# Attention scores through two double-bank buffers in three parts, one maximum a pair, a third score buffer in SBUF

## The chip, the cores and the metric

The kernel runs on one core of a Trainium2 chip. The metric is the device time of one execution in microseconds (us), lower is better. The engines are named as in the profile: PE (matmul) with its weight loads PEld, DVE (vector), ACT (scalar), POOL (GpSimd) and SP, which here only issues DMAs. Each has a queue of its own that runs in order.

## What is computed

A banded attention (8 heads, 4 batches, sequence 768, head size 64) feeds a soft mixture of experts (8 experts with 4 slots each). All in float32, cut to what matters:

```python
def _attn_ref(q, k, v, n_global, n_local):
    scores = scale * np.matmul(q, k.transpose(0, 1, 3, 2))
    rel = pos[:, None] - pos[None, :]
    is_global = pos[None, :] < int(n_global)                 # n_global = 8
    is_local = (rel >= 0) & (rel < int(n_local))             # n_local = 96
    dist = np.where(is_global & ~is_local, float(n_local), np.abs(rel).astype(np.float32))
    scores = np.where(is_global | is_local, scores - slopes[:, None, None] * dist, -1000000000.0)
    a = np.exp(scores - np.max(scores, axis=-1, keepdims=True))
    a = a / (np.sum(a, axis=-1, keepdims=True) + 1e-09)
    return np.matmul(a, v).astype(np.float32)

def _moe_ref(x, phi, w1, w2):
    logits = x @ phi
    d = softmax(logits, over tokens); slot_input = d.T @ x
    slot_out[e] = np.maximum(slot_input[e] @ w1[e], 0.0) @ w2[e]   # 8 experts, 512 -> 1024 -> 512
    return softmax(logits, over slots) @ slot_out
```

(The two softmaxes of the second function are written out in the original.)

## The kernel before

**Work items.** The attention goes over 16 pairs of heads (`units`, numbered u, four pairs a batch; i is the head in the pair). Keys stand on the 128 partitions in seven blocks j of 8 global and 120 local keys. The columns of a block are the queries that can see it, 216 of them (168 and 48 in the last two), so a head's scores are 1296 columns in float32.

**Steps of a pair.** `load_qk` and `load_v` bring q, k and v (two buffers for q and k, one for v). `v_hi` (POOL) and `v_lo` (DVE) split v into two float16 halves. `scores` (line 518) runs 28 PE instructions, both heads side by side, into two PSUM tiles `sc` of three banks each, one a head. `biased` (line 525, DVE) reads a head's 1296 scores, adds the table of distances, writes a float32 buffer (`tp`, four of them, so two pairs) and keeps each partition's maximum. `max_t` (line 533, PE) transposes the maxima into unused columns of a score bank, `max_r` (lines 537 and 538, DVE) reduces and scales them, `max_b` (line 541, PE) spreads the result over the partitions into the same bank and `max_c` (line 545, ACT) copies it out. `exponential` (line 548, ACT) works in place. `w_hi` (line 551, ACT) casts to float16 and `w_lo` (line 555, POOL, in three thirds) writes the rest, also float16, with one buffer of each kind a head. `values` (line 575, PE) multiplies both halves with both halves of v, 39 matmuls a head, into a single bank `x`. `ev_sum`, `ev_rec`, `ev_mul` (lines 580 to 590, DVE) divide by the sum and write `xn`. `tr` (line 603, PE) transposes into a single bank `m` and `tr_copy` (line 608, ACT) takes it out; `logits` (line 633, PE) multiplies with phi through the same bank.

**Once a batch** (u = 3, 7, 11, 15) the strip steps turn the logits into running softmax weights over the tokens and dispatch the batch's tokens to the slots. **After the last pair** come the end of that softmax, the experts' hidden layer (line 106), the projection (line 136), and the combination with the output DMAs.

**Order.** All engines' order comes from one list `ORDER` of steps, written out by hand: each step issues its instructions at its place, and every engine takes its own in that order. `piece` and `free` in that list load the experts' weights: twelve whole pieces of 1 MB into places of their own, the rest into buffers as the attention frees them.

**PSUM before** has eight banks: six for the two score tiles, one for `x`, one for `m`. The lines that keep the maxima in the score banks are

```python
nc.tensor.matmul(out=sc[1][0:2, 1 + z, BW:BW + 64], lhsT=mx, rhs=ident[:, 64 * z:64 * z + 64], start=True, stop=True)
...
nc.vector.tensor_reduce(out=mr, in_=sc[1][0:2, 1:3, BW:BW + 64], axis=AX.XY, op=ALU.max)
```

Of the kernel before, what the change touches and what calls it, by code (L numbers as in the profile page):

```python
# [35 lines left out]
TW = 3 * BW  # L36
PB = KB + P
# [28 lines left out]

# [140 lines left out]
class BiasTable:  # L207
# [66 lines left out]


@with_exitstack
def tile_attention_moe(ctx: ExitStack, tc: tile.TileContext, qk, v, phi, w1, w2, nn, out):
    nc = tc.nc
    const = ctx.enter_context(tc.tile_pool(name="const", bufs=1))
    fast = ExitStack()  # L280
    keep = fast.enter_context(tc.tile_pool(name="keep", bufs=1))
    wk = fast.enter_context(tc.tile_pool(name="wk", bufs=2))
    att = ExitStack()
    ap = att.enter_context(tc.tile_pool(name="ap", bufs=1))
    banks = ExitStack()
# [35 lines left out]
    by_head = "p (j i d) -> p j i d"
    vraw = vt[:, 0:VC].rearrange(by_head, j=NJ, i=2)
    VV = VH + VC // 2
    vhi = [v16[:, VV * i:VV * i + VH].bitcast(F16).rearrange(by_head, j=NJ, i=2) for i in range(2)]
    vlo = [v16[:, VV * i + VH:VV * i + VV].bitcast(F16).rearrange(by_head, j=NJ, i=2) for i in range(2)]
    tabs = [t[:, a:a + TABW].bitcast(BF16).rearrange("p (i c) -> p i c", i=2) for t, a in ((tt, 0), (tt, TABW), (xtt, S), (vt, VC))]
    tbuf = [t[:, 0:TW] for t in tps]
    phi_ = [t[:, TW:].bitcast(F16) for t in tps[0:2]]
    plo_ = [t[:, TW:].bitcast(F16) for t in tps[2:4]]
    xnb = [a[0:KB].rearrange("p (t f) -> p t f", t=NJ) for a in (xn01[:, 0:XH], xn01[:, XH:], xn2[:, 0:XH])]  # L330
    xtb = [xta[:, 0:S], xta[:, S:2 * S], xtt[:, 0:S]]

# [12 lines left out]
    npl = len(places)
    extras = []
    for k, n in enumerate(held):
        at = 0
        for c0, c1 in sorted(c for h, *cs in spaces for c in cs if h == n) + [(WP, WP)]:
            if at < c0:  # L350
                extras.append((NW + k, at, c0))
            at = c1
# [23 lines left out]
    def free(i):  # L376
        n, *cs = spaces[i]
        for c0, c1 in cs:
            load_w([NW + held.index(n)], c0, c1)

# [33 lines left out]
    def blocks(w):  # L414
        return w[:, 0:6 * PB].rearrange("p (s c) -> p s c", c=PB)


    wp = psm.tile([P, 512], F32, name="wp", tag="m")
    busy_in = nc.const_aps.tensor(1.0, [P, 512], BF16)
    for _ in range(WARM):  # L420
        nc.tensor.matmul(out=wp[0:1], lhsT=busy_in[:, 0:1], rhs=busy_in, start=True, stop=True)
# [7 lines left out]
    for i in range(2):  # L429
        nc.gpsimd.memset(vhi[i][:, :, :, D:D + 1], V_SC)  # L430
        for w in (phi_[i], plo_[i]):
            nc.gpsimd.memset(blocks(w)[:, :, QW:], 0.0)
            nc.gpsimd.memset(w[:, 6 * PB:], 0.0)
# [7 lines left out]

    bsel = keep.tile([P, P], F32, name="bsel")
    mms = [keep.tile([P, 2], F32, name=f"mm{i}") for i in range(2)]
    nc.gpsimd.memset(bsel, 0.0)
    nc.gpsimd.memset(bsel[0:3], P_EXP * float(np.log(2.0)))
# [661 lines left out]
```

## Time and profile before

| | |
|---|---|
| median of 3 runs | 239.66 us (239.18 to 243.72) |
| profiled execution | 239.53 us, its span 237.6 us |
| mean granted clock of PE | 0.909 |
| busy PE / DVE / ACT / POOL | 185.2 / 156.6 / 120.4 / 118.8 us |
| weight loads of PE | 142.3 us |
| DMA | 61.39 MB, mean 258 GB/s |

The span is the time from the first to the last instruction in the profiled execution; the execution's time has 1.93 us more around it. An engine's busy time counts instructions under way, without waits, semaphores and DMA issues. The attention's first bias pass starts at 11.16 us, the last head's values end near 174 us, and the hidden layer starts near 184.5 us.

### The profile page before, as it was taken

The page shows a single profiled execution, that of the slowest core. Times are in us where ns is not written, and L with a number is a line of the kernel's source. Part 1 is how long each engine was busy: PE and PEld are TensorE (multiplying, and loading weights), DVE is VectorE, ACT ScalarE, POOL GpSimd, SP SyncE. Part 2 cuts the span into 40 slices and gives each one's busy share as a digit, 9 for nine tenths or more (in the row PEclk, how much of TensorE's full clock was granted, in tenths as well). Part 3 has the DMA queues.
Part 4 walks back from the last instruction along what each step waited for, and adds up shares of the span by engine and source line. Part 5 has one row for each costly group of instructions (what it writes and reads, how often), then busy time and mean ns, then how long its engine had stood idle before and what let it go on. Part 6 is the DMA issues. An engine that isn't in the chain of part 4 may idle for free.

```text
span 237.6 us, 6476 instructions
## 1 busy us (share of the span) xinstructions
PE 185.2 (78%) x2676; PEld 142.3 (60%) x2676; DVE 156.6 (66%) x375; ACT 120.4 (51%) x167; POOL 118.8 (50%) x142
## 2 busy tenths in 40 slices
PE   8463869599698887988985987887688999999800
PEld 2453859587586776876864876766555326666600
DVE  4766192966859759669878696796757783524710
ACT  2001553758839557787764796778522155212500
POOL 7310067395959949978984888889300000000000
PEclk9965555999979999999999999997999999999975
DMA  5795784499996967257336168589799699938895
GB/s 159 274 405 196 316 321 179 125 394 349 372 390 194 415 259 242 69 203 251 103 129 217 21 229 290 151 261 304 254 302 393 206 392 400 384 111 278 293 338 169
DMA packets 20630, 61.39 MB, mean 258 GB/s; under 512 B 1904, under 2 KB 9200, under 8 KB 19056
## 3 DMA queue, kind: packets, MB, share of 16 engines
q1 hardware_dynamic: 20448, 60.89, 71.8%
q8 instruction: 23, 0.38, 0.6%
q14 instruction: 15, 0.12, 0.1%
q10 hardware_dynamic: 144, 0.00, 0.0%
HBM read 54.59 MB, written 6.29 MB: 256 GB/s over the span
## 4 chain that ended last, share of the span: by engine, by line
PE 45%; DVE 29%; issue 8%; POOL 7%; DMA 4%; ACT 2%; DVEq 0%; POOLq 0%; SPq 0%
PE sc L518 17%; DVE tp L525 13%; PE op L136 6%; PE hp L106 6%; PE x L575 6%; DVE v L497 5%; POOL tp L555 4%; DMA vt<-in_v_dram 3%; PE sc L533 2%; PE m L603 2%; DVE mr L537 2%; PE ctp L170 2%; DMA out_dram<-tp 1%; DVE rc L584 1%; DVE mm L538 1%
## 5 line engine op out<-in xcount | busy, mean ns | idle before, releaser
L555 POOL TENSOR_TENSOR tp<-tp 128x432 f16<-128x432 f32 x45 | 49.7, 1132 | 25.2 <-DVE tp L562 17.5
L555 POOL TENSOR_TENSOR tp<-tp,tp 128x432 f16<-128x432 f32 x44 | 49.0, 1140 | 12.7 <-ACT tp L551 8.4
L575 PEld LDWEIGHTS <-tp 128*128 128x128 f16 x1248 | 45.3, 102 | 13.7 <-DVE xmax L590 11.1
L575 PE MATMUL x<-v,tp 128*128 128x65 f16 (+1 forms) x1209 | 46.0, 199 | 8.9 <-DVE xmax L590 8.1
L518 PE MATMUL sc<-raw 64*128 64x216 f32 (+2 forms) x448 | 47.0, 365 | 1.6 <-DMA raw<-in_qk_dram 1.6
L518 PEld LDWEIGHTS sc<-raw 64*128 64x128 f32 x448 | 44.4, 212 | 5.2 <-DMA raw<-in_qk_dram 2.5
L548 ACT ACTIVATE tp<-tp,nb 128x1296 f32<-128x1296 f32 x32 | 44.1, 1377 | 0.6
L551 ACT CAST tp<-tp 128x1296 f16<-128x1296 f32 x30 | 38.2, 1274 | 7.0 <-PE x L575 6.2
L537 DVE TENSOR_REDUCE mr<-sc 2x1 f32<-2x128 f32 x16 | 4.5, 278 | 32.4 <-PE sc L518 32.4
L525 DVE CUSTOM_DVE_ANT_1 tp<-sc,tt 128x1296 f32<-128x1296 f32 x16 | 23.8, 1498 | 1.0 <-POOL tp L555 0.9
L603 PE MATMUL m<-ident,xn 120*128 120x120 f32 x109 | 17.8, 281 | 8.4 <-DVE xmax L590 6.1
L490 POOL TENSOR_SCALAR v<-vt 128x896 f16<-128x896 f32 x16 | 15.0, 940 | 14.5 <-DMA vt<-in_v_dram 12.2
L608 ACT COPY xta<-m 128x480 f32<-128x480 f32 (+1 forms) x21 | 10.1, 480 | 20.4 <-PE m L603 20.3
L590 DVE CUSTOM_DVE_ANT_1 xn<-x,rc 120x448 f32<-120x448 f32 x31 | 19.3, 623 | 1.0
L497 DVE SCALAR_TENSOR_TENSOR v<-vt,v 128x896 f16<-128x896 f32 x16 | 18.4, 1150 | 1.2 <-POOL v L490 1.2
L603 PEld LDWEIGHTS m<-ident,xn 120*128 120x128 f32 x109 | 11.3, 143 | 10.9 <-issue 4.9
L545 ACT COPY nb<-sc 128x2 f32<-128x2 f32 x16 | 2.6, 161 | 28.5 <-DVE mx L525 20.0
L533 PE MATMUL sc<-ident,mx 128*2 128x64 f32 x64 | 7.0, 239 | 8.6 <-DVE mx L525 8.1
L541 PE MATMUL sc<-mm,bsel 128*128 128x2 f32 x32 | 6.3, 266 | 8.2 <-DVE mm L538 7.3
L525 DVE CUSTOM_DVE_ANT_1 tp<-sc,xtt 128x1296 f32<-128x1296 f32 x8 | 12.0, 1499 | 0.5 <-POOL tp L555 0.4
L525 DVE CUSTOM_DVE_ANT_1 tp<-sc,vt 128x1296 f32<-128x1296 f32 x8 | 12.0, 1497 | 0.0
L541 PEld LDWEIGHTS sc<-mm,bsel 128*128 128x128 f32 x32 | 5.2, 203 | 11.2 <-DVE mm L538 8.4
(191 smaller groups left out, 263.6 us busy)
## 6 DMA issues: line engine op xcount, KB each, us to landing
raw<-in_qk_dram SPq DMA_DIRECT2D x15, 832.0 KB, 5.5
wp<-in_w_dram SPq DMA_DIRECT2D x12, 1024.0 KB, 9.5
vt<-in_v_dram SPq DMA_DIRECT2D x16, 448.0 KB, 4.1
wp<-in_w_dram SPq DMA_DIRECT2D x8, 512.0 KB, 8.3
wp<-in_w_dram SPq DMA_DIRECT2D x16, 256.0 KB, 5.4
out_dram<-tp SPq DMA_DIRECT2D x8, 512.0 KB, 6.7
tp<-in_w_dram SPq DMA_DIRECT2D x4, 648.0 KB, 5.5
out_dram<-vt SPq DMA_DIRECT2D x4, 512.0 KB, 4.2
```

Of the source, the lines that this page charges most:

```text
L106: nc.tensor.matmul(out=hp[n][32 * s:32 * s + 32, :], lhsT=slv(a, c, s), rhs=w1(e, c // 2)[:, (c % 2) * DF + 512 * n:(c % 2) * DF + 512 * n ...
L136: nc.tensor.matmul(out=o[32 * s:32 * s + 32, 0:w], lhsT=ht[:, c, 32 * s:32 * s + 32], rhs=w2(4 * a + s, half)[:, c0 + c * w:c0 + c * w + w ...
L490: nc.gpsimd.tensor_scalar(out=vhi[u % 2][:, :, :, 0:D], in0=vraw, scalar1=V_SC, scalar2=0.0, op0=ALU.mult, op1=ALU.add)
L497: nc.vector.scalar_tensor_tensor(out=vlo[k].rearrange("p j i d -> p (j i) d"), in0=vraw.rearrange("p j i d -> p (j i) d"), scalar=V_SC, in ...
L518: nc.tensor.matmul(out=sc[i][:, bk, at:at + n], lhsT=r_[r, KCOL[j]:KCOL[j] + KR], rhs=r_[r, KW + KB * j:KW + KB * j + n], start=True, stop ...
L525: nc.vector.tensor_tensor_reduce(out=tb(u, i).rearrange("p (k c) -> p k c", k=3), in0=sc[i][:, :, 0:BW], in1=table.banks(2 * (u % NP) + i) ...
L548: nc.scalar.activation(out=tb(u, i), in_=tb(u, i), func=AF.Exp, bias=nbs[u][:, i:i + 1], scale=T_SC)
L551: nc.scalar.copy(out=blocks(phi_[i])[:, :, 0:QW], in_=tb(u, i).rearrange("p (s c) -> p s c", c=QW))
L555: (engine or nc.gpsimd).tensor_tensor(out=blocks(plo_[i])[:, c, 0:QW], in0=tb(u, i).rearrange("p (s c) -> p s c", c=QW)[:, c], in1=blocks( ...
L575: nc.tensor.matmul(out=x[:, (D + 1) * t:(D + 1) * t + d], lhsT=w[:, c:c + P], rhs=vv[:, j, i, 0:d], start=(z == 0), stop=(z == len(ops) - ...
L590: nc.vector.tensor_tensor_reduce(out=xnb[(u // 2) % 3][:, :, c:c + D], in0=xps.pop((u, i))[:, :, 0:D], in1=rcs.pop((u, i)).unsqueeze(2).to ...
L603: nc.tensor.transpose(out=m[:, at:at + KB], in_=xnb[(u // 2) % 3][:, t, P * (p % 2):P * (p % 2) + P], identity=ident[0:KB, 0:KB])
```

## The change

**PSUM.** The six score banks become four: two buffers of two banks, a bank for each head. `scores(u, k)` writes a third of a pair's columns (blocks 0 and 1; 2 and 3; 4 to 6) of both heads into the buffer whose turn it is, and `biased(u, k)` takes that third of both heads out in one instruction of 2 x 432 columns. The two banks left over give `values` a bank for each head (`x0`, `x1`) and give transposes, logits, dispatch and the maxima two banks that go round (`bank()`).

**Maximum.** The running maximum of the three bias parts is one for both heads; one PE transposition into an `m` bank, one DVE reduction straight into the operand of the broadcast, one column copied out. The scaling instruction of line 538 is gone.

**SBUF.** Three float32 buffers of a whole pair (`NTB = 3`) take the place of two pairs' worth. The float16 buffers stay at one a head (`NHB = 1`), v's raw buffer at one. All attention buffers now lie in one block of twelve weight places, so `free` loads slices that cross places.

**Order.** `ORDER` is new. Every second `v_hi` is on ACT (`v_hi_act`, pairs 0, 2, 4 and so on to 14). Nine warm matmuls stand behind the first pair's scores. The first slice of q and k is loaded first; the twelve weight pieces come in another order. The third batch's strip steps stand in the last pair instead of at pairs 13 and 14.

The core of the diff:

```diff
+NTB = 3
+NHB = 1
...
-    sc = [pss.tile([P, 3, 512], F32, name=f"sc{i}", tag=f"sc{i}") for i in range(2)]
...
+    def bank():
+        turn[0] += 1
+        return psm.tile([P, 512], F32, name="m", tag=f"m{turn[0] % 2}")
...
-    def scores(u):
+    def scores(u, k):
 
+        scs[u, k] = sc = pss.tile([P, 2, 512], F32, name="sc", tag=f"s{(3 * u + k) % 2}")
         r_ = rq[u % 2]
-        for j in range(NJ):
-            bk = next(k for k in range(3) if j in BANK_J[k])
-            n, at = QN[j], COL[j] - BW * bk
+        for j in BANK_J[k]:
+            n, at = QN[j], COL[j] - BW * k
             for i in range(2):
                 r = slice(D * i, D * i + D)
-                nc.tensor.matmul(out=sc[i][:, bk, at:at + n], lhsT=r_[r, KCOL[j]:KCOL[j] + KR],
+                nc.tensor.matmul(out=sc[:, i, at:at + n], lhsT=r_[r, KCOL[j]:KCOL[j] + KR],
                                  rhs=r_[r, KW + KB * j:KW + KB * j + n], start=True, stop=True)
...
-    def biased(u, i):
+    def biased(u, k):
...
-            out=tb(u, i).rearrange("p (k c) -> p k c", k=3), in0=sc[i][:, :, 0:BW], in1=table.banks(2 * (u % NP) + i),
-            scale=1.0, scalar=-3.0e38, op0=ALU.add, op1=ALU.max, accum_out=mxs[u][:, i:i + 1])
+            out=tbs[u % NTB].rearrange("p (i c) -> p i c", i=2)[:, :, BW * k:BW * k + BW], in0=scs.pop((u, k))[:, :, 0:BW], in1=table.part(u % NP, k),
+            scale=1.0, scalar=mxs[u][:, k - 1:k] if k else -3.0e38, op0=ALU.add, op1=ALU.max, accum_out=mxs[u][:, k:k + 1])
 
     def max_t(u):
-        mx = mxs.pop(u)
-        for z in range(2):
-            nc.tensor.matmul(out=sc[1][0:2, 1 + z, BW:BW + 64], lhsT=mx, rhs=ident[:, 64 * z:64 * z + 64], start=True, stop=True)
+        ms[u, "m"] = m = bank()
+        nc.tensor.matmul(out=m[0:1, 0:P], lhsT=mxs.pop(u)[:, 2:3], rhs=ident, start=True, stop=True)
 
     def max_r(u):
-        mr = wk.tile([2, 1], F32, name="mr", tag="mr", bufs=2)
-        nc.vector.tensor_reduce(out=mr, in_=sc[1][0:2, 1:3, BW:BW + 64], axis=AX.XY, op=ALU.max)
-        nc.vector.tensor_scalar(out=mms[u % 2][0:2], in0=ident[0:2, 0:2], scalar1=mr, scalar2=None, op0=ALU.mult)
+        nc.vector.tensor_reduce(out=mms[u % 2][0:1], in_=ms[u, "m"][0:1, 0:P], axis=AX.X, op=ALU.max)
...
     def values(u, i):
-        x = bank(("values", u, i))
+        xps[u, i] = x = psx.tile([P, 512], F32, name="x", tag=f"x{i}")
```

What the new order does is seen in three places.

DVE at the start of the program. `xn` is here the workspace of the distance tables, `tt` (before) and `wa` (after) hold the finished table, and `wa` after the change holds all attention buffers. Before:

```order
L250 SCALAR_TENSOR_TENSOR xn_107<-nv,xn_107 8x1
L497 SCALAR_TENSOR_TENSOR v_101<-vt,v_101 128x896
L255 TENSOR_SCALAR xn_107<-xn_107 8x216
L256 COPY tt<-xn_107 128x216
L257 CAST xn_107<-xn_107 8x216
L258 TENSOR_TENSOR tt<-xn_107 8x216
L259 COPY tt<-xn_107 128x432
L261 COPY tt<-xn_107 128x168
L261 COPY tt<-xn_107 128x48
L270 TENSOR_SCALAR tt<-tt 128x864
L525 ISA tp_98,mx<-sc_177,tt 128x1296
```

The same place after the change:

```order
L263 SCALAR_TENSOR_TENSOR xn_96<-nv,xn_96 8x1
L268 TENSOR_SCALAR xn_96<-xn_96 8x216
L269 COPY wa<-xn_96 128x216
L270 CAST xn_96<-xn_96 8x216
L271 TENSOR_TENSOR wa<-xn_96 8x216
L272 COPY wa<-xn_96 128x432
L274 COPY wa<-xn_96 128x168
L274 COPY wa<-xn_96 128x48
L283 TENSOR_SCALAR wa<-wa 128x864
L545 ISA wa,mx<-sc,wa 128x2x432
L545 ISA mx 128x1
L524 SCALAR_TENSOR_TENSOR wa<-wa 128x896
```

The low half of v (128x896) has moved from ahead of the table to behind the first bias part.

DVE in the middle of the attention, from one pair's reduction of the maxima (TENSOR_REDUCE) on. Before:

```order
L537 TENSOR_REDUCE mr<-sc_177 2x1
L538 TENSOR_SCALAR mm_163<-ident,mr 2x2
L497 SCALAR_TENSOR_TENSOR v_101<-vt,v_101 128x896
L525 ISA tp_97,mx<-sc_176,xtt 128x1296
L525 ISA mx 128x1
L580 TENSOR_TENSOR rsall<-x,eps 120x7
L584 RECIPROCAL rc<-rsall 120x7
L590 ISA xn_106,xmax<-x,rc 120x7x64
L590 ISA xmax 120x1
L525 ISA tp_98,mx<-sc_177,xtt 128x1296
```

After:

```order
L555 TENSOR_REDUCE mm_152<-m 1x1
L610 RECIPROCAL rc<-rsall 120x7
L616 ISA xn_96,xmax<-x,rc 120x7x64
L616 ISA xmax 120x1
L524 SCALAR_TENSOR_TENSOR wa<-wa 128x896
L545 ISA wa,mx<-sc,wa,mx 128x2x432
L545 ISA mx 128x1
L606 TENSOR_TENSOR rsall<-x,eps 120x7
L610 RECIPROCAL rc<-rsall 120x7
L616 ISA wa,xmax<-x,rc 120x7x64
L616 ISA xmax 120x1
L545 ISA wa,mx<-sc,wa,mx 128x2x432
```

The reduction reads a bank `m` of its own kind instead of a score tile, nothing scales its result, and bias parts stand singly between the divisions of the values.

PE in the same stretch, up to the next head's values. Before, the transposition of the maxima (line 533) and ten rows of scores of 216 columns stand right ahead of these:

```order
L518 MATMUL sc_176<-raw_95 128x168
L518 MATMUL sc_177<-raw_95 128x168
L518 MATMUL sc_176<-raw_95 128x48
L518 MATMUL sc_177<-raw_95 128x48
L603 MATMUL m<-ident,xn_107 128x120 x4
L541 MATMUL sc_177<-mm_163,bsel 128x2
L575 LDWEIGHTS tp_97
L575 MATMUL x<-v_101,tp_97 128x65
```

After, with the transposition as the first row:

```order
L552 MATMUL m<-ident,mx 1x128
L535 MATMUL sc<-wa 128x216 x4
L558 MATMUL m<-mm_152,bsel 128x1
L535 MATMUL sc<-wa 128x216 x2
L535 MATMUL sc<-wa 128x168 x2
L535 MATMUL sc<-wa 128x48 x2
L599 LDWEIGHTS wa
L599 MATMUL x<-wa 128x65
```

A pair's scores no longer stand in one piece: the broadcast of the maximum lies between parts, and parts are spread among the values of two heads.

More of the change, by code (lines that the diff above doesn't have):

```diff
@@ new lines, in tile_attention_moe, with home @@
+    VW = VHW + VC // 2
+    used, blocks = {}, []
+    def home(name, n, **parts):
+        t = keep.tile([P, n * WP], F32, name=name)
+        blocks.extend((t, WP * k) for k in range(n))
+        at, views = 0, {}
+        for k, w in parts.items():
+            used[k] = (t, at, at + w)
+            views[k] = t[:, at:at + w]
+            at += w
+        assert at <= n * WP, (name, at)
+        return views
+    home_of = {}
+    for name, n, parts in homes(QKW=QKW, TBW=TBW, HPW=HPW, VC=VC, VW=VW, TABW=TABW, XH=XH):
+        home_of.update(home(name, n, **parts))
@@ new lines, in tile_attention_moe @@
+    vraw = own("vraw", VC).rearrange(by_head, j=NJ, i=2)
+    v16 = [own(f"v{i}", VW) for i in range(2)]
+    vhi = [w[:, 0:VHW].bitcast(F16).rearrange(by_head, j=NJ, i=2) for w in v16]
+    vlo = [w[:, VHW:].bitcast(F16).rearrange(by_head, j=NJ, i=2) for w in v16]
+    xn2 = own("xn2", XH)
+    xnb = [a[0:KB].rearrange("p (t f) -> p t f", t=NJ) for a in (xn01[:, 0:XH], xn01[:, XH:], xn2)]
+    xtb = [own(f"xt{i}", S) for i in range(3)]
+    last = nu - 1
+    spaces = []
+    for name in leaves:
+        t, a, b = used[name]
+        spaces.append([(k, max(a, at) - at, min(b, at + WP) - at) for k, (bt, at) in enumerate(blocks) if bt is t and max(a, at) < min(b, at + WP)])
@@ L342, in tile_attention_moe @@
         if name == "free":
-            held = [n for n in held if n != spaces[i][0]] + [spaces[i][0]]
-    places = weights + [holders[n] for n in held]
+            for k, *_ in spaces[i]:
+                held = [n for n in held if n != k] + [k]
+    places = weights + [blocks[k][0][:, blocks[k][1]:blocks[k][1] + WP] for k in held]
     npl = len(places)
@@ L412, in tile_attention_moe, with blocks_of, warm @@
     ones = keep.tile([P, P], F32, name="ones")
-    def blocks(w):
-        return w[:, 0:6 * PB].rearrange("p (s c) -> p s c", c=PB)
-    wp = psm.tile([P, 512], F32, name="wp", tag="m")
+    def blocks_of(w, i):
+        return w[:, PW * i:PW * i + 6 * PB].rearrange("p (s c) -> p s c", c=PB)
+    turn = [0]
+    def bank():
+        turn[0] += 1
+        return psm.tile([P, 512], F32, name="m", tag=f"m{turn[0] % 2}")
+    wp = bank()
     busy_in = nc.const_aps.tensor(1.0, [P, 512], BF16)
-    for _ in range(WARM):
-        nc.tensor.matmul(out=wp[0:1], lhsT=busy_in[:, 0:1], rhs=busy_in, start=True, stop=True)
+    def warm(u, n):
+        for _ in range(n):
+            nc.tensor.matmul(out=wp[0:1], lhsT=busy_in[:, 0:1], rhs=busy_in, start=True, stop=True)
+    warm(0, WARM)
     table = BiasTable(nc, tabs, xn01)
@@ L496, in v_lo @@
         k = u % 2
-        nc.vector.scalar_tensor_tensor(out=vlo[k].rearrange("p j i d -> p (j i) d"), in0=vraw.rearrange("p j i d -> p (j i) d"), scalar=V_SC,
-                                       in1=vhi[k].rearrange("p j i d -> p (j i) d")[:, :, 0:D], op0=ALU.mult, op1=ALU.subtract)
-    idb = ident.bitcast(BF16)
-    def busy(to):
-        for n in (256, 256, P):
-            nc.tensor.matmul(out=to[:, 0:n], lhsT=idb[:, 0:P], rhs=idb[:, 0:n], start=True, stop=True)
-    def warm_x(u):
-        busy(psx.tile([P, 512], F32, name="x", tag="x"))
@@ L621, in logits @@
         if units[u][1] % 2:
-            ms[u] = bank(("logits", u))
+            ms[u] = bank()
             logits_of(u, 1)
@@ L716, in dispatch @@
     def dispatch(b):
-        ms[b, "s"] = m = bank(("dispatch", b))
+        ms[b, "s"] = m = bank()
         for k in range(2):
@@ L744, in tile, with warm @@
             return left.tile([P, 512], F32, name="ld", tag="x")
-        warm()
+        idle = left.apart(0)
+        def warm():
+            for n in (256, 256, P):
+                nc.tensor.matmul(out=idle[0:1, 0:n], lhsT=busy_in[:, 0:1], rhs=busy_in[:, 0:n], start=True, stop=True)
         warm()
@@ L814, in tile_attention_moe @@
     left = LeftBanks()
[L815 removed]
+    last_dispatch(left)
     att.close()
```

182 lines of the change are left out of this document (88 added, 94 removed).

## Prediction

> **What bounds the kernel now.** I read the windows by stage first, with borders at the times that the chain of waits gives; columns are the length, busy microseconds (instructions) of PE, its weight loads, DVE, ACT, POOL, then the granted clock, the DMA share and GB/s.
>
> ```profile
> 14.25:33.63 19.38, 14.14 (x107) 12.66 (x107) 10.15 (x18) 5.62 (x6) 2.21 (x2) 0.50 0.74 288
> 33.63:76.55 42.92, 34.35 (x547) 29.86 (x547) 30.36 (x67) 28.32 (x33) 32.34 (x32) 0.88 0.77 291
> 76.55:160.22 83.67, 69.65 (x1224) 58.91 (x1224) 65.93 (x159) 58.77 (x79) 68.54 (x64) 1.00 0.60 204
> 177.70:237.60 59.90, 46.12 (x536) 26.61 (x536) 28.78 (x76) 16.86 (x33) 0.00 (x0) 0.92 0.83 297
> ```
>
> The third row is the steady stage. Nine reductions of a maximum lie in it (the row of line 537 below), so nine pairs, 9.30 us each. Per pair PE is busy 7.74 us, POOL 7.62, DVE 7.33, ACT 6.53: no engine is full, so something makes them take turns. The chain of waits (start, length, piece) says what, and the list of waits how much; the last two lines are line 537's own answer for that stage.
>
> ```profile
> 104.63 2.49 PE sc L518 x28
> 107.14 0.29 DVE mr L537
> ...
> 109.19 1.42 DVE tp L525
> ...
> 111.60 1.42 DVE tp L525
> ...
> 113.08 0.39 PE sc L533 x4
> DVE mr L537 <- PE sc L518: 32.4, 15, 4.0
> PE x L575 <- DVE xmax L590: 8.1, 7, 2.0
> DVE tp L525 <- POOL tp L555: 1.3, 3, 0.4
> L537 DVE TENSOR_REDUCE mr<-sc x9: 279/279/280, 79.5 to 153.3; 2x1 f32<-2x128 f32 x9
>   PE sc L518: 15.6, 9
> ```
>
> PE transposes a pair's maxima into a score bank, then fills the same banks with the next pair's 28 score matmuls; the reduction that reads those maxima starts when all 28 are done, and everything behind it on DVE stands. That is 32.4 us in all and 15.6 in the steady stage, 1.73 a pair. Then both bias passes must end before PE may fill the banks again. One loop goes through DVE and PE once a pair.
>
> **The frame of the sum.** Three points of the timeline and a start:
>
> ```profile
> 22.82 1.38 ACT L548 ACTIVATE tp<-tp,nb 128x1296 f32<-128x1296 f32 x1
> 29.55 0.28 DVE L537 TENSOR_REDUCE mr<-sc 2x1 f32<-2x128 f32 x1 [3.42 <-PE sc L518]
> 31.91 1.72 PE L575 MATMUL x<-v,tp 128*128 128x65 f16 x28 [0.50 <-DVE tp L555]
> 171.42 1.35 PE L575 MATMUL x<-v,tp 128*128 128x65 f16 x39
> span 237.6 us, 6476 instructions
> ```
>
> The first head's values end at 33.63, the same head of the last pair at 172.77: 139.14 us for 15 pairs, 9.28 each. Behind that lie 64.83 us. The profiled execution took 239.53 us, 1.93 more than its span, and the median of the runs is 239.66; I count against the profiled one.
>
> **Start.** Up to the first exponential the change takes a step off DVE and adds warm matmuls:
>
> ```profile
> 6.78 0.20 DVE L250 SCALAR_TENSOR_TENSOR xn<-nv,xn 8x1 f32<-8x1 f32 x1
> 8.17 1.09 DVE L497 SCALAR_TENSOR_TENSOR v<-vt,v 128x896 f16<-128x896 f32 x1 [1.20 <-POOL v L490]
> 9.18 0.32 DVE L255 TENSOR_SCALAR xn<-xn 8x216 f32<-8x216 f32 x1
> 14.77 4.83 PE L518 MATMUL sc<-raw 64*128 64x216 f32 x28
> L421 PE MATMUL wp<-const-bfloat16-1.0 128*1 128x512 bf16 x12 | 5.3, 627 | 0.8 <-PEq L1096 0.8
> ```
>
> The table steps waited for the low half of v. It now stands behind the first bias part, so tables start at 6.98 instead of 9.18 and the first bias at about 9.0. Three parts of 0.98 (below), v_lo and one table copy of about 0.5 put the next pair's first part at 13.5. On PE the first pair's third score part ends near 11.4, nine warm matmuls cost 9 x 0.44 = 4.0 at the clock of the row (12 in 5.3), and the next scores' first part 8/28 of 4.83 = 1.4 at half clock: 16.8. Transpose, reduction, broadcast and copy add about 2, so the first exponential stands at 19 rather than 22.82 (at full clock all of this PE work halves: 16.3). From there to the first values the old kernel took 10.81, 3.42 of which was DVE's wait for scores that the change removes: 7.4. So 26.4 at half clock, 23.7 at full; I take **25.5**, nearer the half-clock rows, with 23.7 and 28 (the old start, less two thirds of the 8 us) as ends.
>
> **Per pair, part by part.**
>
> ```profile
> L525 DVE CUSTOM_DVE_ANT_1 tp<-sc,tt 128x1296 f32<-128x1296 f32 x16 | 23.8, 1498 | 1.0 <-POOL tp L555 0.9
> L590 DVE CUSTOM_DVE_ANT_1 xn<-x,rc 120x448 f32<-120x448 f32 x31 | 19.3, 623 | 1.0
> L538 DVE TENSOR_SCALAR mm<-ident,mr 2x2 f32<-2x2 f32 x16 | 10.1, 634 | 0.6
> L533 PE MATMUL sc<-ident,mx 128*2 128x64 f32 x64 | 7.0, 239 | 8.6 <-DVE mx L525 8.1
> L490 POOL TENSOR_SCALAR v<-vt 128x896 f16<-128x896 f32 x16 | 15.0, 940 | 14.5 <-DMA vt<-in_v_dram 12.2
> L497 DVE SCALAR_TENSOR_TENSOR v<-vt,v 128x896 f16<-128x896 f32 x16 | 18.4, 1150 | 1.2 <-POOL v L490 1.2
> L551 ACT CAST tp<-tp 128x1296 f16<-128x1296 f32 x30 | 38.2, 1274 | 7.0 <-PE x L575 6.2
> L555 POOL TENSOR_TENSOR tp<-tp 128x432 f16<-128x432 f32 x45 | 49.7, 1132 | 25.2 <-DVE tp L562 17.5
> ```
>
> *Bias in three.* Two shapes of the same operation, 1498 ns for 1296 columns and 623 for 448, give 1.03 ns a column, so 864 columns take 1.05 us. The chain counts 1.42 for a pass, since the next starts before it has drained, so a part occupies 0.97 to 0.98. Three parts are 2.93 against 2.84: +0.09 us of DVE; bounds 0 and +0.3 (no overlap between parts, which now read the running maximum of the part before).
>
> *One maximum a pair.* The 634 ns scaling goes from DVE, and of the four transposing matmuls (0.39 together) two: -0.2 on PE. *Scores in three calls:* 28 matmuls as before; three starts instead of one cost 0 to 0.3, I take 0.1.
>
> *Half of v's high part on ACT.* POOL loses 0.94 in every second pair. ACT is not shown doing it; 1274 ns for 1296 columns give 0.88 for 896, so +0.45 us a pair, bounds 0.4 and 0.7.
>
> Loads per pair then: PE 7.65, POOL 7.15, ACT 7.0, DVE 6.8. *Two value banks* take away PE's 8.1 us of waits for the evacuation, *the third float32 buffer* at most 1.3 (the row of DVE waiting for POOL). Both lie in PE's or DVE's idle time and come out as the ability to run ahead, not as terms.
>
> **What is late next.** The loop over DVE and PE is gone; three others stay. The float16 weights still have one buffer a head: cast 1.27, three differences 3 x 1.13, values 1.36, then the next cast: 6.0, under PE's load. The raw v still has one buffer: load, high part, low part, next load.
>
> ```profile
> vt<-in_v_dram SPq DMA_DIRECT2D x16, 448.0 KB, 4.1
> DMA to landing us min/median/max: 3.2/4.1/6.3
> ```
>
> That is 4.1 + 0.94 + 1.15 = 6.2 us, and about 8.3 when both steps find one instruction of 1.1 us ahead of them; with the slowest landing 10.5. And each score part waits on PE, in order, for the bias part two before it; behind it in PE's queue stand the values and transposes, and for those wait ACT's next cast and POOL's differences. PE at 7.65 with idle of 9% instead of today's 17% gives the same 8.4. So **8.4 us a pair**; bounds are 7.65 (PE never waits) and 9.28 (nothing gained).
>
> **End.** In the new order the third batch's strip steps (maximum, to tokens, dispatch) stand in the last pair instead of two pairs earlier, and the transposes of pair 14 behind the last values.
>
> ```profile
> L712 PE MATMUL m<-xn,dn 120*32 120x256 f32 x84 | 5.8, 382 | 0.0
> 204.17 8.38 PE op L136 x148
> ```
>
> A third of these 84, 1.9 us, plus a transpose, partly beside DVE's work: +1.5, bounds 0 and 3. The loads are the same bytes in another order, with about one whole weight piece a pair early on as before; but 1.4 MB of small leftovers, which came behind v's loads in mid-kernel, now come with the freed buffers, and those freed behind the last pair's first values hold 5.5 MB instead of 3.8 (both counted from the slices in the code). Of the 1.6 MB more the price is 4.5 us if nothing hid it (the last window moved 297 GB/s at a share of 0.83, so 358 at full share), but the projection that needs these weights starts at 204.17, 31 us behind those values: 0.
>
> **Sum.** 25.5 + 15 x 8.4 + 64.83 + 1.5 = 217.8; with 1.93 the execution takes **220 us**, 8% less. The start gives 8.1 of the 20 us, the pairs 13.2, the end takes 1.5.
>
> **Rivals.** *A: another wait takes the place of the old one.* PE is held at the two score buffers, or v lands late, as the DMA share of 0.77 before 76.55 grows to 0.85 when the same bytes come in 8.4 us a pair: the pair stays at 9.28. For it: v's bare loop plus queueing is near 8.3 already, and four queues in order are now coupled three times a pair. Against: 1.73 us a pair of pure DVE standing goes. Only start and end count: 25.5 + 139.1 + 64.8 + 1.5 + 1.9 = **233**. *B: the engines pack up to PE's load:* 15 x 7.65 instead of 8.4, **209**. For it: three pairs in flight. Against: four loads within 0.9 us of each other and all queues in order. *C, slower: the clock.* Between 14.25 and 33.63 PE was busy 73% of the time and got a clock of 0.50:
>
> ```profile
> 34.79 2.31 PE L575 MATMUL x<-v,tp 128*128 128x65 f16 x39 [1.16 <-DVE xmax L590]
> ```
>
> There a head's values took 2.31 instead of 1.35 and scores 4.83 instead of 2.49. If the short waits at the score buffers brought that back, a pair would cost 8.4 + 2.3 + 2 x 0.96 = 12.6; from six of the fifteen pairs on, the kernel is slower than before by over 2% (220 + 6 x 4.2 = **245**). Against it: in the steady stage PE idles 17% of the time and still had 1.00, and this change shortens that. [...] *D: the change doesn't do what it says:* the maxima now share two banks with transposes and logits, and the reduction waits for ACT to empty them instead of for the scores. If the old 1.73 stays and ACT, with 0.45 us more a pair, sits in the loop, a pair takes 9.7: 25.5 + 146 + 64.8 + 1.5 + 1.9 = **240**, within 2%.
>
> **How the numbers follow.** Forecast (213 to 229) 0.62, A 0.15, B 0.12, C 0.07, D 0.04. What a measurement of this kernel can tell from no change is about 2%, 235 to 244. Faster: the forecast, B and most of A, 0.85; within: the rest of A and D, 0.08; slower: C, 0.07. The range takes in the pair's two bounds and so A's and B's times: 209 to 234.
>
> **What would show it.** Steps right: line 555's reduction (the old 537) has no score matmul among its releasers; exponential of the first pair near 16 to 19 us; values of the last pair near 151; PE the busiest engine of the steady window at about 90%; clock 1.00 there. Wrong: waits of PE's score matmuls for DVE of over half a microsecond a part or of POOL and ACT for v's DMA (A), a clock under 0.9 after 40 us (C), the reduction waiting for ACT's copies (D), or an end longer than 68 us behind the last pair's first values.

## The result, and the profile after

| | before | after |
|---|---|---|
| median of 4 runs, side by side | 239.42 us (236.57 to 243.72) | 216.07 us (212.17 to 220.56) |
| ratio | | 0.893, 95% interval 0.876 to 0.910 |
| profiled execution, its span | 239.53 us, 237.6 us | 213.78 us, 211.8 us |
| first and last reduction of a maximum start at | 19.6 and 160.8 us | 17.3 and 133.7 us |
| reduction to reduction, mean of 15 | 9.41 us | 7.76 us |

The change is faster by about 11%; the forecast for the profiled execution was 220 us, and it took 213.78. (Some executions are longer, most at a lower granted clock, two of the kernel after by 2 to 4% at 0.942 and 0.952 against 0.971 and 0.976; ratios, here and below, leave them out, and the profiles of the kernel before and of the two kernels with one value bank are of such longer executions.) The last two rows give a measure that every kernel below shares: its 16 reductions, one a pair, divide the span into a start, 15 pairs and an end. By it the start gives 2.3 of the 25.8 us of span, the pairs 24.8, and the end takes 1.3 back (from the last reduction 76.8 us before, 78.1 after).

The windows by stage of the kernel after; columns as in the prediction (length, then busy time of PE, its weight loads, DVE, ACT and POOL, granted clock, DMA share, GB/s):

```profile
25.00:42.00 17.00, 13.80 (x233) 11.65 (x235) 15.33 (x36) 12.80 (x15) 13.98 (x13) 1.00 0.99 379
42.00:60.00 18.00, 15.88 (x263) 12.97 (x263) 15.11 (x37) 14.06 (x16) 15.70 (x16) 1.00 0.90 333
60.00:133.00 73.00, 72.55 (x1220) 59.10 (x1218) 64.50 (x162) 61.91 (x84) 65.57 (x61) 1.00 0.70 248
```

And line 555, the old 537, in the third of these stages, with what DVE waited for ahead of it:

```profile
L555 DVE TENSOR_REDUCE mm<-m x9: 272/279/280, 62.6 to 127.0; 1x1 f32<-1x128 f32 x9
  PE m L552: 0.2, 1
```

The 32.4 us that this reduction waited for scores are gone, and no score matmul is among its releasers. From 62.6 to 127.0 us lie eight pairs, 8.05 us each. In the steady stage the engines hardly take turns any more: PE is busy 72.55 of 73 us. The load of the nine pairs whose reductions lie there is, a pair, PE 8.06, POOL 7.29, DVE 7.17, ACT 6.88. The chain of waits of that stage says the same, piece by piece (start, length, engine, line, number of matmuls):

```profile
62.25 0.31 PE m L552 x2
62.56 0.93 PE sc L535 x8
63.49 0.31 PE m L558 x2
63.80 0.46 PE m L628 x3
64.26 1.00 PE sc L535 x12
65.26 1.28 PE x L599 x39
66.54 0.93 PE sc L535 x8
...
73.42 3.78 POOL wa L583 x3
...
89.64 2.47 POOL wa L583 x3
...
94.27 2.84 POOL wa L583 x2
```

Twice in 73 us the chain runs through POOL's differences, from 73.4 to 77.2 and from 89.6 to 97.1 us, with PE busy nearly all the while; all else is PE after PE. A pair's scores stand in three pieces, 0.93 + 0.93 + 1.00 = 2.86 us, where the chain before had 2.49 in one.

Ahead of 60 us it is not so. PE is idle 3.2 of 17 and 2.1 of 18 us, at a DMA share of 0.99 and 0.90, and the chain has this:

```profile
42.97 7.43 DMA wa<-in_qk_dram
50.41 0.14 issue
50.54 1.00 PE sc L535 x8
51.54 0.01 PE m L628
51.55 7.50 DMA wa<-in_qk_dram
```

Loads of q and k, issued when the scores two pairs earlier have let go of their buffer, land 7.4 to 7.5 us later (5.5 was the median before, 6.8 is now), and the next scores follow at once. In a second profile of the same kernel ("after, again" below) PE was idle 3.9 of these 35 us and its scores waited less than a microsecond for such loads, so this part of the account belongs to the first profile.

The points of the prediction's frame, from the timeline:

```profile
18.28 1.38 ACT L565 ACTIVATE wa<-wa,nb 128x1296 f32<-128x1296 f32 x1
23.83 1.02 PE L599 MATMUL x<-wa 128*128 128x65 f16 x28 [0.81 <-DVE wa L583]
143.32 1.67 PE L599 MATMUL x<-wa 128*128 128x65 f16 x50 [0.28 <-DVE xmax L616]
```

The first exponential starts at 18.28; the first head's values end at 24.85; 39 of the 50 matmuls of the last row are the same head of the last pair, which therefore ends near 144.6.

### The profile page after: what moved, and what is told of

The parts are those of the page before. It is cut to its first block, busy times and chain, and to the rows that moved or that the text cites. A ratio compares the mean times of both kernels' runs of the same rounds, so it can differ in the third digit from the quotient of the medians.

```text
span 211.8 us, 6473 instructions
## 1 busy us (share of the span) xinstructions
PE 181.9 (86%) x2650; PEld 130.8 (62%) x2650; DVE 155.1 (73%) x391; ACT 125.0 (59%) x175; POOL 111.7 (53%) x131
## 4 chain that ended last, share of the span: by engine, by line
PE 52%; DMA 9%; POOL 6%; DVE 5%; ACT 2%; issue 2%; DVEq 0%; POOLq 0%; SPq 0%
PE sc L535 12%; PE x L599 11%; DMA wa<-in_qk_dram 7%; PE a L149 7%; PE hp L119 7%; POOL wa L583 6%; PE m L628 5%; DMA out_dram<-wa 2%; PE m L658 2%; PE ctp L183 2%; PE m L552 1%; PE cp L209 1%; PE m L558 1%; PE ld L737 1%; PE htp L133 1%
## 5 line engine op out<-in xcount | busy, mean ns | idle before, releaser
L583 POOL TENSOR_TENSOR wa<-wa 128x432 f16<-128x432 f32 x89 | 99.5, 1148 | 19.5 <-DVE wa L579 10.8
L535 PE MATMUL sc<-wa 64*128 64x216 f32 (+2 forms) x448 | 49.0, 344 | 6.4 <-DMA wa<-in_qk_dram 3.3
L599 PE MATMUL x<-wa 128*128 128x65 f16 (+1 forms) x1248 | 44.3, 193 | 3.9 <-POOL wa L583 2.8
L599 PEld LDWEIGHTS <-wa 128*128 128x128 f16 x1248 | 41.1, 97 | 8.8 <-issue 4.1
L575 ACT CAST wa<-wa 128x1296 f16<-128x1296 f32 x30 | 38.1, 1270 | 12.5 <-PE x L599 10.8
L535 PEld LDWEIGHTS sc<-wa 64*128 64x128 f32 x448 | 36.6, 186 | 13.4 <-issue 4.3
L565 ACT ACTIVATE wa<-wa,nb 128x1296 f32<-128x1296 f32 x32 | 43.9, 1377 | 0.3
L545 DVE CUSTOM_DVE_ANT_1 wa<-sc,wa,mx 128x864 f32<-128x864 f32 x32 | 35.6, 1112 | 2.6 <-PE sc L535 1.3
L524 DVE SCALAR_TENSOR_TENSOR wa<-wa 128x896 f16<-128x896 f32 x16 | 23.2, 1449 | 1.8 <-ACT nb L562 1.6
L545 DVE CUSTOM_DVE_ANT_1 wa<-sc,wa 128x864 f32<-128x864 f32 x16 | 16.8, 1052 | 2.6 <-PE sc L535 2.2
```

The costliest lines, as they stand in the source:

```text
L524: nc.vector.scalar_tensor_tensor(out=vlo[k].rearrange(flat), in0=vraw.rearrange(flat), scalar=V_SC, in1=vhi[k].rearrange(flat)[:, :, 0:D], ...
L535: nc.tensor.matmul(out=sc[:, i, at:at + n], lhsT=r_[r, KCOL[j]:KCOL[j] + KR], rhs=r_[r, KW + KB * j:KW + KB * j + n], start=True, stop=True)
L545: nc.vector.tensor_tensor_reduce(out=tbs[u % NTB].rearrange("p (i c) -> p i c", i=2)[:, :, BW * k:BW * k + BW], in0=scs.pop((u, k))[:, :, ...
L565: nc.scalar.activation(out=head(u, i), in_=head(u, i), func=AF.Exp, bias=nbs[u], scale=T_SC)
L575: nc.scalar.copy(out=h, in_=t)
L583: (engine or nc.gpsimd).tensor_tensor(out=w, in0=t, in1=h, op=ALU.subtract)
```

## The experiments

All are of the kernel after unless their name begins with b (before). The reductions are those of the profiled execution; "a pair" is their mean distance.

| kernel | median (range) us | span us | first, last reduction | a pair |
|---|---|---|---|---|
| maxima apart (b) | 228.43 (227.03 to 230.56) | 225.1 | 15.6, 148.4 | 8.85 |
| scores broken (b) | 244.44 (one run) | 242.5 | 21.3, 166.7 | 9.69 |
| after, again | 213.88 (211.78 to 217.38) | 213.1 | 15.7, 133.2 | 7.83 |
| PE less | 211.58 (208.71 to 217.63) | 206.8 | 15.7, 127.6 | 7.46 |
| POOL less | 215.25 (213.35 to 216.08) | 212.6 | 17.4, 133.9 | 7.77 |
| one value bank | 225.78 (219.68 to 226.85) | 224.4 | 17.4, 143.3 | 8.39 |
| the same, dispatch ahead | 225.12 (219.96 to 226.87) | 225.1 | 17.4, 143.5 | 8.41 |
| v's high half on POOL | 218.77 (217.37 to 219.81) | 218.0 | 18.0, 137.3 | 7.95 |
| no warm matmuls | 213.75 (212.16 to 217.34) | 212.7 | 15.6, 134.7 | 7.94 |
| pieces later | 217.84 (216.85 to 218.87) | 216.8 | 15.7, 138.4 | 8.18 |
| pieces even | 214.94 (214.83 to 215.25) | 213.0 | 15.7, 134.8 | 7.94 |
| pieces behind v | 213.79 (212.49 to 215.44) | 212.0 | 17.4, 131.7 | 7.62 |

### The removed wait alone: before, with the maxima in a bank of their own

```diff
     def max_t(u):
+        ms[u, "m"] = bank(("max", u))
-            nc.tensor.matmul(out=sc[1][0:2, 1 + z, BW:BW + 64], lhsT=mx, ...)
+            nc.tensor.matmul(out=ms[u, "m"][0:2, 64 * z:64 * z + 64], lhsT=mx, ...)
     def max_r(u):
-        nc.vector.tensor_reduce(out=mr, in_=sc[1][0:2, 1:3, BW:BW + 64], axis=AX.XY, op=ALU.max)
+        nc.vector.tensor_reduce(out=mr, in_=ms.pop((u, "m"))[0:2, 0:P], axis=AX.X, op=ALU.max)
```

(Three `tr_copy` steps and one `max_r` stand a few places earlier, so that the one bank is free in time.)

> The kernel before with one thing changed: the pair's maxima are transposed into the bank of the transposes instead of a score bank, so the reduction no longer waits for the next 28 score matmuls (32.4 us in all before, 1.73 us a pair). Theory 1, the prediction's: that wait was the loop that set the pair; gone by itself it brings 1 to 1.7 us a pair, 15 to 25 us, 0.90 to 0.94 of before. Theory 2: the six score banks are still filled in one piece and PE may not refill them before both bias passes have ended, so the wait turns up elsewhere (PE's scores behind DVE, or DVE's bias behind the scores): under 0.5 us a pair, 0.97 to 1.00 of before; the split into parts is then what the change needs.

Ratio 0.960 (0.952 to 0.968): between the two theories. The reduction's wait fell from 32.4 us to the first row below. Against the profile before, the span is 12.5 us shorter: 4.0 in the start and 0.56 in each of 15 pairs; the medians of the runs side by side differ by 9.9 (238.3 and 228.43).

```profile
  PE m L534: 4.2, 6
```

What PE's values (line 575, here 576) waited for, weight loads counted in, first before and then in this kernel, says why it was not 1.73 a pair:

```profile
  DVE xmax L590: 19.2, 15
```

```profile
  DVE xmax L591: 13.8, 15
  POOL tp L556: 2.8, 3
```

The wait for the division (`ev_mul`) through the one value bank stayed, 13.8 of 19.2 us. In PE's line of the list of waits, which the prediction quoted, it stood with 8.1 us; the other 11.1 stood with the weight loads. Part of what the pairs gained is clock, which was back at 1.00 from about 28 us on, where the kernel before had 0.50 up to 40:

```profile
20.00:28.00 8.00, 4.87 (x34) 4.36 (x34) 5.73 (x10) 4.09 (x4) 1.01 (x1) 0.55 0.81 316
28.00:34.00 6.00, 4.76 (x104) 4.40 (x104) 5.76 (x14) 5.36 (x5) 4.93 (x6) 1.00 0.81 322
```

So the wait that the prediction named is worth between a third and a half of the change by itself: 4.0 of 10.7% by the ratios, 12.5 of 25.8 us by the two profiled spans. The rest came with the other parts of the change, of which the second value bank and v's high half on ACT are taken back singly below.

### One value bank instead of two

```diff
-        xps[u, i] = x = psx.tile([P, 512], F32, name="x", tag=f"x{i}")
+        xps[u, i] = x = psx.tile([P, 512], F32, name="x", tag="x0")
```

> The kernel after with a single bank for the values of both heads; fourteen division steps stand a little earlier in the order, so that each head's division comes ahead of the next head's values. Theory 1: now that PE is full in the steady stretch (72.55 of 73 us), each wait of a head's values for the division of the head before comes on top, as the 13.8 us of waits for the division in the kernel before with only the maxima moved: 5 to 12 us more than the kernel after, a pair 8.3 to 8.6 us between reductions instead of 7.76. Theory 2: scores stand between the values of two heads, so the division is done by then: under 2 us.

> The kernel after with a single bank for the values of both heads, as in the run before, with the third batch's dispatch now ahead of the division of pair 14, whose buffer it reads (in the run before it stood behind it, so that run's dispatch read pair 14's rows). Theory 1: PE waits some 15 us for divisions (14.9 us, 15 times, in the run before, 0.3 us in the kernel after), and 5 to 10 us of it come on top: 0.91 to 0.94 of the kernel before where the kernel after is at 0.883 to 0.893; a pair takes 8.2 to 8.4 us between reductions instead of 7.8. Theory 2: the run before was long for its low clock (0.921) alone; here 2 us or less are left.

The first of the two computes something else: its third batch's dispatch reads rows of pair 14. Their times agree: 8.39 and 8.41 us a pair, a span of 224.4 and 225.1, and even the shortest runs, 219.68 and 219.96, are above the two profiled ones of the kernel after (213.78 and 214.88). In the second, the values waited as the first theory said, where they waited 0.3 us with two banks:

```profile
  DVE xmax L616: 18.8, 15
```

The second theory, that scores between two heads' values cover the division, is out. A gap of 1.85 us among these waits was followed by a second harm, a lower clock:

```profile
123.10 1.36 PE L599 MATMUL x<-wa 128*128 128x65 f16 x39 [1.85 <-DVE xmax L616]
124.39 0.39 PE L552 MATMUL m<-ident,mx 128*1 128x128 f32 x2
124.71 1.81 PE L535 MATMUL sc<-wa 64*128 64x216 f32 x8
```

```profile
121.00:124.00 3.00, 1.15 (x33) 0.93 (x32) 1.98 (x6) 1.78 (x3) 2.02 (x3) 1.00 0.85 305
124.00:127.00 3.00, 3.00 (x30) 2.15 (x26) 2.11 (x6) 1.27 (x1) 2.44 (x3) 0.61 0.63 212
127.00:130.00 3.00, 3.00 (x20) 2.14 (x22) 2.52 (x5) 1.73 (x3) 3.00 (x3) 0.50 0.50 143
130.00:133.00 3.00, 3.00 (x57) 1.94 (x50) 0.16 (x1) 1.73 (x4) 0.22 (x1) 0.76 0.03 13
```

Soon behind the gap PE had half its clock for 6.8 us, and a score part took 1.81 us instead of 1.00. In all the first profile has 17.1 us at half clock between 42 and 133 us (a mean of 0.81 from 42 to 60 and 0.93 from 60 on), the second 10.2 between 25 and 133 (0.90 from 25 to 42 and 0.95 from 60 on); the two profiles of the kernel after have 1.00 from 25 to 145. A score part took 1.8 times as long at half clock, so this can explain at most half of these stretches, 8.5 and 5.1 us, of the 11 to 13 us by which the spans are longer. The shortest run of each had a mean clock of 0.969 and 0.967, close to the 0.971 and 0.972 of the profiled runs of the kernel after, and is still 5 to 6 us above those: that is an estimate of the bank alone, from one run of each.

### Less work on PE, less work on POOL

```diff
-                    for w, vv, d in ((ph, vh, D + 1), (ph, vl, D), (pl, vh, D + 1)):
+                    for w, vv, d in ((ph, vh, D + 1), (pl, vh, D + 1)):
```

> The kernel after without the product of the high half of the weights with the low half of v: 26 of 78 value matmuls a pair are left out, about 0.85 us of PE a pair (a head's 39 took 1.28 us in the steady stretch). Theory 1: PE alone sets the pace from 60 to 133 us (busy 72.55 of 73 us, nine pairs, 8.1 us each); a pair falls to what POOL (7.29 us a pair) and DVE (7.17) allow, 7.4 to 7.6 us, and the whole to 207 to 211 us. Theory 2: the order of the queues makes the engines take turns and a full PE is only its symptom: less than 2 us gained, 214 or more, with PE at about 90% there.

```diff
-('w_lo', u, i, 1) for every head that has it on POOL (30 of 32)
+nc.vector.memset(blocks_of(wlo[0], i)[:, 2:4, 0:QW], 0.0), once
```

> The kernel after without the middle third of the low half of the weights (it stays zero after one clearing at the start): two of six differences a pair are left out, 2.3 us of POOL's 7.29 us a pair. Theory 1 (PE alone sets the pace): 0 to 1.5 us gained in all, since POOL stands in the chain of the steady stretch only twice. Theory 2 (the engines take turns, POOL at 90% among them): 5 us or more gained, 209 or less.

The stretch from 60 us, first with less PE, then with less POOL:

```profile
60.00:130.00 70.00, 66.37 (x964) 51.23 (x961) 64.25 (x165) 62.84 (x85) 65.61 (x60) 1.00 0.72 251
```

```profile
60.00:130.00 70.00, 68.89 (x1150) 55.69 (x1150) 61.05 (x155) 59.61 (x81) 45.17 (x40) 1.00 0.69 246
```

A third of POOL's work taken away brings nothing: 7.77 us a pair against 7.76 to 7.83, PE still 98% busy. Leaving out a third of the value matmuls brings 0.3 to 0.4 us a pair of the 0.85 removed, and then POOL is at 94%, DVE at 92% and PE at 95%. Both fit "PE sets the pace, with POOL and DVE close behind"; by times alone the first is less sure, since its ratio, 0.887 (0.880 to 0.894), overlaps that of the unchanged kernel.

### What a break between score matmuls costs

```diff
+            if j in ((1, 3) if u % 2 else (6, 6)):
+                for _ in range(1 if u % 2 else 2):
+                    nc.tensor.matmul(out=sc[0][0:1, 0, BW:BW + 64], lhsT=idb[:, 0:1], rhs=idb[:, 0:64], start=True, stop=True)
```

> The kernel before with two small bf16 matmuls (64 columns into unused columns of a score bank) in every pair: in odd pairs one behind the first and one behind the second score bank, in even pairs both behind all 28 score matmuls. Otherwise nothing is changed. Theory 1: PE pays for every break between score matmuls and other work; in the kernel after the three parts take 0.93, 0.93 and 1.00 us, 2.86 together, in the chain of waits against 2.49 for the 28 in one piece. Then from the first score matmul to the end of the last of the 30 instructions PE takes 0.3 us or more longer in odd pairs than in even ones. Theory 2: a break costs nothing by itself and the parts are long for another reason: under 0.1 us of difference.

PE's timeline for one odd pair and the even one behind it:

```profile
97.73 1.00 PE L518 MATMUL sc<-raw 64*128 64x216 f32 x8
98.66 0.19 PE L522 MATMUL sc<-ident 128*1 128x64 bf16 x1
98.78 1.00 PE L518 MATMUL sc<-raw 64*128 64x216 f32 x8
99.71 0.19 PE L522 MATMUL sc<-ident 128*1 128x64 bf16 x1
99.83 1.07 PE L518 MATMUL sc<-raw 64*128 64x216 f32 x12
100.84 0.63 PE L606 MATMUL m<-ident,xn 120*128 120x120 f32 x4
...
106.97 2.54 PE L518 MATMUL sc<-raw 64*128 64x216 f32 x28
109.44 0.22 PE L522 MATMUL sc<-ident 128*1 128x64 bf16 x2
109.59 0.63 PE L606 MATMUL m<-ident,xn 120*128 120x120 f32 x4
```

From the first score matmul to the transposes behind it: 100.84 - 97.73 = 3.11 us broken, 109.59 - 106.97 = 2.62 us whole, with the same 30 instructions. Two breaks cost 0.49 us, 0.25 each, and the couple at 137.13 and 147.12 us shows the same 3.11 and 2.62. Theory 1 holds. Of the 0.49, the scores' own stretches make 0.40 (0.93 + 0.93 + 1.01 against 2.47), close to the 0.37 that the three parts cost in the chain of the kernel after; there the breaks are between other matmuls, and their price was not taken apart.

### Every high half of v on POOL

```diff
-('v_hi_act', u) for u = 0, 2, ... 14
+('v_hi', u)
```

> The kernel after with every high half of v on POOL again (ACT had those of the even pairs): POOL gets 0.47 us a pair more (7.29 to 7.75 in the steady stretch), ACT 0.48 less. Theory 1: PE sets the pace there, so the move is worth nothing as long as POOL stays under 8.06: within 1.5 us of the kernel after. Theory 2: POOL already stands in the chain of waits twice (73.4 to 77.2 and 89.6 to 97.1 us) and is the engine next in line; 2 to 6 us more.

Ratio 0.913 (0.906 to 0.921), 0.883 and 0.893 being the kernel after, which did not run beside this one: the move to ACT is worth some 5 us by the medians (218.77 and 213.88), and theory 1 is wrong here, though POOL's load stays under PE's. Two rows are longer. What PE's values waited for, in the kernel after (8.4 us, 12 times, in its second profile) and in this one:

```profile
  POOL wa L583: 6.1, 10
```

```profile
  POOL wa L583: 10.3, 20
L524 DVE SCALAR_TENSOR_TENSOR wa<-wa x16: 1089/1752/1895, 11.3 to 139.1; 128x896 f16<-128x896 f32 x16
```

The second line is v's low half on DVE, minimum, median and maximum in ns. Its median was 1073 before the change and 1419 in the kernel after, and with a third of POOL's differences left out it was this:

```profile
L526 DVE SCALAR_TENSOR_TENSOR wa<-wa x16: 1073/1094/1926, 10.5 to 135.6; 128x896 f16<-128x896 f32 x16
```

With the change in place the median was higher where POOL was busier: 1094 ns with POOL busy 65% of the stretch from 60 us, 1419 and 1752 with 90%. POOL's load alone does not make it: in the kernel before POOL was busy 82% of the steady stage, 12 of the 16 ran beside line 555 from end to end, and 9 of these took 1.07 us. What makes it slow, and how much of the 5 us comes this way, was not shown.

### The warm matmuls

```diff
-('warm', 0, 9)
```

> The kernel after without the nine warm matmuls behind the first pair's scores (3.74 us of PE from 11.6 to 15.3 us, 0.50 of the clock, which is back at 1.00 by 17 us). Theory 1: they bring the clock back; without them PE keeps 0.50 up to 35 or 40 us, as in the kernel before (0.50 from 14.25 to 33.63 us), the first values end 3 us later or more and the whole takes 3 to 6 us more. Theory 2: they only stand in the way of the next scores: the first reduction stands 1 to 3 us earlier, the clock is near 1.00 from 20 us on all the same, and the whole is 0 to 3 us shorter.

Theory 1 is out and theory 2 is nearer, without its gain. The median, 213.75, is that of the unchanged kernel beside it, 213.88. The first reduction stands at 15.6 us without them, and with them at 17.3 or 15.7, as the clock happened to fall during them or not. Without them PE had half its clock for some 10 of the first 25 us (a mean of 0.80), with them for 3.4 us in one profile (0.93) and not at all in the other (1.00), and yet the first head's values end at 24.4 us against 24.85 and 23.2. From 25 to 42 us the clock is 1.00 here too. So they are not why the long stretch at 0.50 of the kernel before, up to about 40 us, is gone; that was not settled. A kernel before with less waiting (the maxima apart) had its full clock back at 28 us.

### Weight pieces at other places

```diff
-('piece', 2), ('piece', 6), ... where the order has them (pairs 1 to 7)
+ten of the twelve behind loads of pairs 6 to 12
```

(In the order of steps these ten now stand two or three pairs later than they did, and not six as the first text below says.)

> The kernel after with ten of the twelve weight pieces of 1 MB loaded about six pairs later, so that the loads of q and k between 25 and 60 us share the DMA engines with less (share 0.99 and 0.90 there, 0.70 from 60 to 133). Theory 1: the two q and k loads of 7.43 and 7.50 us in the chain of waits are late because of those pieces; they land in 5 us or less, and 3 to 5 us of PE's 5.3 idle us between 25 and 60 go: 209 to 211 in a run like the profiled one, 0.98 of the kernel after. Theory 2: the load is late since it may be issued only when the scores two pairs earlier are done, whatever else is moved: under 1 us. Theory 3: the pieces then make loads late between 60 and 133: slower than the kernel after.

> The kernel after with the twelve weight pieces of 1 MB spread, one behind each load of q and k from pair 2 to pair 13, where the run with ten pieces later gained between 25 and 60 us (PE busy 33.3 of 35 us there instead of 29.7) and lost it at 71 to 82 us, where v's load landed 10.8 us after its issue behind 4 MB of pieces. Theory 1: both loads then land in time, PE is over 95% busy from 25 to 133 us, and 2 to 4 us go against the unchanged kernel beside it. Theory 2: at some 290 GB/s all the way either q and k or v is late again somewhere: within 1 us or slower.

> The kernel after with the weight pieces spread, one a pair from the fourth load of q and k on, each behind the later of that pair's two loads, so that no load of v stands right behind a piece: in the run with one piece behind each load of q and k, the load of v issued at 69.55 us landed 9.42 us later, behind about 3.3 MB issued ahead of it in the same queue. Theory 1: the order in the queue was all; no load of v or of q and k takes over 7 us, PE is over 95% busy from 25 to 133 us and 1 to 3 us go: 211 to 213 us. Theory 2: the bytes themselves are too many for this time, some load is late again: 214 us or more.

The first had PE busy 33.3 us between 25 and 60 us (29.7 and 31.1 in the two profiles of the kernel after), so theory 1 had the gain there right, though a load of q and k still took 6.1 us; it then lost more at one place, as theory 3 had it:

```profile
71.14 10.79 DMA wa<-in_v_dram
```

Behind that wait PE had half its clock from 81.4 to 88.2 us, which is part of the loss. The second had the same at 69.55 us, a little smaller (half clock from 80.6 to 84.0). SP's issues ahead of that load:

```profile
63.23 0.42 SPq L398 DMA_DIRECT2D wp<-in_w_dram  x1
68.62 0.33 SPq L414 DMA_DIRECT2D wa<-in_qk_dram  x1
69.00 0.42 SPq L398 DMA_DIRECT2D wp<-in_w_dram  x1
69.55 11.93 SPq L417 DMA_DIRECT2D wa<-in_v_dram  x2
```

The third removes that place: v's loads land within 5.7 us, PE is busy 96% of the time from 25 to 133 us (95 and 94% in the two profiles of the kernel after), and its last reduction is the earliest of all kernels with the whole work, 131.7 us. Its time is still the same as that of the unchanged kernel, 213.79 and 213.88, because 80.3 us follow that reduction instead of 78 to 80. Part of such a difference between ends is PE's own time for the same work, as at a lower clock: in the second profile of the kernel after (79.9 us) 20 matmuls of the dispatch took 2.49 us from 154.57 on, in the first (78.1 us) 1.43, with the clock at 1.00 from 152 to 156. What these pieces gain is under 1%, and no version that is faster than the kernel after was found.

## Why the prediction was right, and where its steps were not

The forecast of 220 us held near the lower edge of its 213 to 229. That it came as near as it did is partly luck, as two of its steps were wrong in opposite directions. The sum of the prediction against the profile, in us:

| term | predicted | measured |
|---|---|---|
| start, to the end of the first head's values | 25.5 | 24.85 |
| 15 pairs | 126.0 (8.4 each) | 119.75 (7.98 each) |
| end | 66.33 | 67.2 |
| around the span | 1.93 | 1.98 |
| execution | 220 | 213.78 |

**Start.** Right within 0.7 us; the first exponential at 18.28 lies in the 16 to 19 that were given. That warm matmuls cost 4 us at half clock also came out (3.74), but their absence changed nothing that could be measured.

**The pair.** The term was mis-sized by 0.42 us a pair, 6.3 us in all, and that is nearly the whole miss. Two steps failed in opposite directions. *Scores in three calls* were put at +0.1 us a pair with 0.3 as the upper bound; in the chain they cost 0.37 (2.86 against 2.49), and the two breaks by themselves were measured at 0.49, both outside the bound. *One maximum a pair* was to take 0.2 us from PE: in the chain its transposes take 0.31 instead of 0.39, so 0.08. The two make 0.39 of the 0.41 by which PE's load, 8.06 us a pair, is above the 7.65 of the sum. Then *PE with idle of 9%*: PE was idle 0.6% of the steady stage, 3.6% in the second profile of the same kernel (70.34 of 73 us). That is the mechanism of rival B, engines packed up to PE's load, at a load 0.4 us higher than the one B was priced at. Its 209 us would have needed PE's load to stay at 7.65. *Bias in three* took 1.05 us for the first part and 1.11 for the other two, 3.28 against two passes of 1.50: +0.28, under the upper bound of 0.3 but not the 0.09 that was taken. *Half of v on ACT* took 0.95 us each against 0.88, inside the bounds, and it was worth more than its small term suggests: some 5 us when undone. DVE's load came to 7.17 and not 6.8; v's low half, a mean of 1.45 us where the sum had 1.15, is the largest piece of that, and the sum had no term for it.

**Two value banks and the third buffer** were said to be "the ability to run ahead, not terms". For the value bank that was too little: it was sized by PE's 8.1 us of waits, while the values waited 19.2 us with their weight loads counted, and taking the bank away from the kernel after costs 5 to 6 us by the shortest runs. The third float32 buffer was not tried alone.

**What is late next.** The prediction named the float16 buffers, v's buffer and the score buffers. In the chain it was the one place it had not named, the loads of q and k, between 42 and 60 us, where the same bytes came in less time. That is a piece of rival A, in two of sixteen pairs. Score matmuls waited 2.9 us once for DVE, far under the half microsecond a part that would have meant A.

**End.** +2.4 us on the 64.83 instead of +1.5, inside its bounds.

**C and D.** The clock was 1.00 from 25 to 133 us, with three hand-overs of score buffers a pair, and from 60 to 133 us PE's score matmuls waited at none of them. That such waits bring the half clock back was C's premise, and the kernel after did not put it to the test. The single-bank kernel had a clock of 0.50 behind a wait of 1.85 us for a bank, though waits of 1.76 and 2.24 us had no such effect in the kernel after (below). D is out: the reduction waited 0.2 us.

## What to carry to other kernels

When a wait goes, price what stands behind it on the same engines, and count a wait on PE together with that of its weight loads: here the removed wait alone gave a third to a half of the gain, and with one bank for the values the kernel after was slower again. When a step is split, put the price of each break on the engine that will be full: 0.37 us a pair instead of 0.1 was the largest error in PE's load. And undo a cheap-looking helper before calling it slack: POOL at 90% beside PE at 99% still delayed it when it got half a microsecond more a pair.

## What was not expected of the hardware

- Where small bf16 matmuls stood between float32 score matmuls, PE lost about 0.25 us at each of the two breaks (3.11 against 2.62 us for the same 30 instructions).
- An idle gap of PE of 1.85 us was followed by 6.8 us at half clock in the second profile with one value bank (0.61, 0.50 and 0.76 in the three windows from 124 to 133 us). The length of the gap alone does not decide it: the kernel after had a gap of 1.76 us (38.88 to 40.64) and, in its second profile, the one below, and kept 1.00 behind both. What does decide it was not shown.

```profile
72.98 1.29 PE L599 MATMUL x<-wa 128*128 128x65 f16 x37 [2.24 <-POOL wa L583]
```

- A load landed late behind what was issued ahead of it on SP's queue: in the kernel with even pieces v's 448 KB took 9.42 us behind pieces and q and k that make 3.3 MB with it, and 3.0 us at the least elsewhere in the same run (median 4.1).
